# Own weight loads for some Q and K products, so that a group of four segments holds 4,096 TensorE instructions

## The chip, the cores and the metric

The kernel runs on one core of one Trainium2 chip. The metric is the device time of one execution in microseconds (us), as a median over several executions. TensorE executes the matrix products, and here it has two kinds of instruction: a matmul (PE in the profile) and the load of a weight block into the array (PEld). VectorE is DVE, ScalarE is ACT, GpSimd is POOL, and SyncE (SP) issues nearly all DMAs.

## The reference

Two independent branches are computed over 2,048 rows of width 640 and mixed by a gate. Branch A is attention with a recurrent memory: 64 segments of 32 rows, in which every segment sees 8 memory rows ahead of its own 32, and the first 8 output rows of a segment become the memory of the next one. Branch B is a gated MLP.

```python
for s in range(n_seg):                       # 64 segments, one after the other
    h = jnp.concatenate([mem, xs], axis=1)   # 8 + 32 rows
    q, k, v = (jnp.einsum('btd,dhe->bhte', h, W) for W in (Wq, Wk, Wv))   # 32 heads of 192
    p = softmax(where(mask, q @ k.T * scale, -1e9))
    o = jnp.einsum('bhte,hed->btd', p @ v, Wo)
    mem = o[:, :M, :]
    outs.append(o[:, M:, :])
b = (gelu(x @ w_gate) * (x @ w_up)) @ w_down
return g * a + (1 - g) * b                   # g = sigmoid(sum(x * gate_w))
```

(The loop's lines are shortened.) The last 8 rows of each segment can't reach the memory of the next one. The kernel calls them the left rows and computes them for four segments at once.

## The kernel before, in words

The kernel first runs branch B over four blocks of 512 rows (`ffn_gu`, `ffn_down`, lines 829 to 885) and stores its result to DRAM. It then computes the left rows' Q and K products for the first units (`left_mm`, line 917), and then the 64 segments (`segment`, line 1462).

Everything is recorded by a small scheduling layer (`_Sched`), which keeps one instruction list for each engine in the order of recording and puts in semaphore waits. The order within a segment is written by hand in three tables (`PROG`, `PROG1`, `PROG3`); a segment takes table `s % 4`, so the program repeats every four segments. Four segments are called a group; there are 16 groups. There is no loop in the machine program: all instructions are laid out one behind another, and each engine's list is fetched from DRAM while it runs.

A Q, K or V product of one segment (`proj`, line 1116) is done in octets of 8 heads and in 5 steps over the contraction (k = 0 to 4). One step of one octet is four matmuls: the stationary operand is the same 128x32 block of the segment's rows (`htile(k)`), and the four matmuls go to the four 32-column strips of the array (j = 0 to 3), each with 384 columns of the weight matrix as the moving operand. Where two or three products of one step stand behind one another they share that stationary block. So only the first of them loads it (line 1138, four weight loads and four matmuls); the others are issued with `ldweights=False` by `_matmul_kept` (line 226, four matmuls without a load). For the left rows, `left_mm` does the same: its Q product loads (line 930) and its K product keeps (line 226).

The other TensorE work of a segment: the scores (lines 1187 to 1202 and 234), the transposes of the probabilities (1249, 1254), the products with V (1282, 1284) and the output projection, in halves of 320 columns (1338), 160 columns for the last octet (1364), and 320 columns with 64 stationary columns in the fourth segment of a group (1383). The memory rows come back from the output projection through DVE: an add (line 1580) and two transposes (line 1583), for which the first K product of the next segment waits.

Of the kernel before, what the change touches and what calls it, by code (L numbers as in the profile page):

```python
# [223 lines left out]
def _matmul_kept(e, out, lhsT, rhs, like, stop):  # L224
    nm = e.bass.get_next_instruction_name()
    return e.add_instruction(mybir.InstMatmult(  # L226
        name=nm, start_tensor_calc=like["start"], stop_tensor_calc=stop, tile_size=(128, 32),
        tile_position=like["tile_position"], ldweights=False,
        ins=[e.lower_ap(rhs), e.lower_ap(lhsT)], outs=[e.lower_ap(out)]))
# [9 lines left out]
def _build(nc, A_x, A_mem0, A_Wq, A_Wk, A_Wv, A_Wo, seg_len, w_gate, w_up, w_down,  # L239
# [282 lines left out]
    def piece_view(key, o):  # L522
        if key[0] == 3:
            return bview(o, GO).rearrange("p (c n) -> p c n", n=Dm)
        return bview(o, GQ)
# [34 lines left out]
    def octet(s, i):  # L560
        return i if s % 2 == 0 else NOCT - 1 - i
# [5 lines left out]
    def group_at(item):  # L567
        return GROUPS[item[1]][::-1] if item[1:] == (0, 0) else GROUPS[item[1]]
# [69 lines left out]
    def piece(seg, key):  # L638
        order = orders[seg % 4]
        oi = last_req.get(seg, -1) + 1  # L640
        assert order[oi] == key, "pieces must be consumed in order"
        last_req[seg] = oi
        if seg == 0 and key in tmp_off:
            return left_piece(key)
        if seg and key == (EM, octet(seg, 0), EK):
            return None, None
        done_keys.append(key)
        return piece_view(key, res_off[key]), r_res[key]
# [164 lines left out]
    def htile(k):  # L813
        return XB[:, k, :]
# [98 lines left out]
    S_.add("pool", lambda e: e.memset(Qz, 0.0), writes=[r_Qz])  # L913
    lb = {}
    LBK = {}

    def left_mm(g, o, k, src):
        keys = [(m, o, k) for m in range(2)]
        for m, key in enumerate(keys):
            g_, rg_ = src(key)  # L920
            lhs = XLg[g % 2][:, k, :]
            fns = []
            for j in range(4):
                outp = ps[32 * j:32 * j + 32, LBK[m], 0:384].rearrange("p (c i) -> p c i", i=32)
                rhs = ek_j[j].rearrange("p (c i) -> p c i", i=32) if g_ is None else g_.rearrange("p (c j i) -> p j c i", c=12, j=4)[:, j]
                if m:
                    fns.append(lambda e, outp=outp, rhs=rhs, j=j: _matmul_kept(
                        e, outp, lhs, rhs, dict(start=(k == 0), tile_position=(0, 32 * j)), k == KT - 1))
                else:
                    fns.append(lambda e, outp=outp, rhs=rhs, j=j: e.matmul(  # L930
                        outp, lhs, rhs, start=(k == 0), stop=(k == KT - 1), tile_position=(0, 32 * j)))
            S_.add("pe", fns, reads=([rg_] if rg_ else r_ek) + [r_XLg[g % 2]], writes=[r_ps[LBK[m]]], name="L%s g%d o%d k%d" % ("QK"[m], g, o, k))

    def left_rows(g, o, m, bk, dst, rd, rowl, r_rowl):
        S_.add("act", lambda e: e.activation(out=rowl, in_=ps[:, bk, 0:384], func=ACTF.Copy),
               reads=[r_ps[bk]], writes=[r_rowl], name="L rows g%d o%d" % (g, o))
        S_.add("dve", lambda e: e.transpose(out=dst.rearrange("p q c i -> p c q i"), in_=rowl.rearrange("p (c r) -> p c r", r=L)),
               reads=[r_rowl], writes=rd, name="L T%s g%d o%d" % ("qk"[m], g, o))
# [20 lines left out]
    def vl_evac(s, o, bk, eng="dve"):  # L959
        out, in_ = vl_sb[o].rearrange("p (c n) -> p c n", c=3), ps[:, bk, 0:384].rearrange("p (n c) -> p c n", c=3)  # L960
        if eng == "act":
            S_.add("act", lambda e: e.activation(out=out, in_=in_, func=ACTF.Copy),
                   reads=[r_ps[bk]], writes=[r_vl[o]], name="Vl evac s%d o%d" % (s, o))
        else:
            S_.add("dve", lambda e: e.tensor_copy(out=out, in_=in_),
                   reads=[r_ps[bk]], writes=[r_vl[o]], name="Vl evac s%d o%d" % (s, o))
# [10 lines left out]
    for n, (g, o) in enumerate(units):  # L977
        b = n % 4
        for m in range(2):
            LBK[m] = ((3, 4), (0, 1), (2, 7))[n % 3][m]  # L980
        for k in range(KT):
            left_mm(g, o, k, left_piece)
        for m in range(2):
            left_rows(g, o, m, LBK[m], lst[b][:, :, m], [r_lst[b]], rows_sb[m], r_rows[m])
        if g == 0:
# [120 lines left out]
    def misc_bank(s, group=9):  # L1106
        tick[0] += 1
        ok = [b for b in (0, 1, 2, 3) + ((LB,) if s % 4 in (1, 2) or s % 4 == 3 and group < 3 else ()) + ((OB,) if group < (1, 3, 3, 9)[s % 4] else ()) if b not in bk_of.values() and b not in lb.values()]
        b = min(ok, key=lambda b: misc[b])
        misc[b] = tick[0]  # L1110
        return b
# [4 lines left out]
    def proj(s, item):  # L1116
        ms = GROUPS[item[1]]
        k = item[2]
        if k == 0:
            for mi in ms:  # L1120
                bk_of[mi] = LB if s % 4 == 0 and item[1] == 2 and mi[0] == 0 else misc_bank(s, item[1])
                if mi[0] == 2 and s % 4 == 0 and mi[1]:
                    bk_of[(3, mi[1])] = OB if mi[1] == 1 else LB

        def mms(m, bk, lhs, k, g_, keep):
            fns = []
            for j in range(4):
                outp = ps[32 * j:32 * j + 32, bk, 0:384]
                if m < 2:
                    outp = outp.rearrange("p (c i) -> p c i", i=32)  # L1130
                    rhs = ek_j[j].rearrange("p (c i) -> p c i", i=32) if g_ is None else g_.rearrange("p (c j i) -> p j c i", c=12, j=4)[:, j]
                else:
                    rhs = g_[:, 384 * j:384 * (j + 1)]
                if keep:
                    fns.append(lambda e, outp=outp, rhs=rhs, j=j: _matmul_kept(
                        e, outp, lhs, rhs, dict(start=(k == 0), tile_position=(0, 32 * j)), k == KT - 1))
                else:
                    fns.append(lambda e, outp=outp, rhs=rhs, j=j: e.matmul(  # L1138
                        outp, lhs, rhs, start=(k == 0), stop=(k == KT - 1), tile_position=(0, 32 * j)))
            return fns  # L1140

        for n, (m, i) in enumerate(group_at(item)):
            o, bk = octet(s, i), bk_of[(m, i)]
            g_, rg_ = piece(s, (m, o, k))
            S_.add("pe", mms(m, bk, htile(k), k, g_, n > 0),
                   reads=([rg_] if rg_ else r_ek) + [r_Hm[int(k >= KA[1])], r_HxT], writes=[r_ps[bk]],
                   name="%s s%d o%d k%d" % ("QKV"[m], s, o, k))
        for m, i in ms:
            if m == 2 and s % 4 == 0 and i:
                o, bk = octet(s, i), bk_of[(3, i)]  # L1150
                g_, rg_ = piece_view((2, o, k), res_off[(2, o, k)]), r_res[(2, o, k)]
                S_.add("pe", mms(2, bk, XLg[s // 4 % 2][:, k, :], k, g_, False),
                       reads=[rg_, r_XLg[s // 4 % 2]], writes=[r_ps[bk]], name="Vl s%d o%d k%d" % (s, o, k))
        if k < KT - 1:
            return
        for m, i in ms:
            o, bk = octet(s, i), bk_of[(m, i)]
            if m < 2:
                S_.add("act", lambda e, m=m, bk=bk: e.activation(out=rows_sb[m], in_=ps[:, bk, 0:384], func=ACTF.Copy),  # L1159
                       reads=[r_ps[bk]], writes=[r_rows[m]], name="rows evac")  # L1160
                continue
            S_.add("act", lambda e, i=i, bk=bk: e.activation(out=v_sb[i % NVB].rearrange("p (c n) -> p c n", c=3),  # L1162
                                                             in_=ps[:, bk, 0:384].rearrange("p (n c) -> p c n", c=3), func=ACTF.Copy),
                   reads=[r_ps[bk]], writes=[r_v[i % NVB]], name="V evac s%d o%d" % (s, o))
            if s % 4 == 0 and i:
                vl_evac(s, o, bk_of[(3, i)])
        tick[0] += 1
        for bk in bk_of.values():
            misc[bk] = tick[0]
        bk_of.clear()  # L1170
# [290 lines left out]

    def segment(s):
        g, q = s // 4, s % 4
        post = []
        n_wo, nqkv = n_wos[q], nqkvs[q]
        for n, item in enumerate(PROGS[q]):
# [24 lines left out]
            elif kind == "lf":  # L1491
                if i == q and unit(s, item[2]):
# [3 lines left out]
                    for m in range(2):  # L1496
                        LBK[m] = lb[item[2], m]
                    left_mm(*unit(s, item[2]), item[3], unit_piece)
# [97 lines left out]
    for s in range(NSEG):  # L1596
        segment(s)
# [79 lines left out]
```

## Time and profile before

| what | value |
|---|---|
| median of 3 runs | 1651.25 us (1649.93 to 1654.85) |
| span of the profiled execution | 2114.2 us; the page shows no time around the span |
| granted TensorE clock in the profiled execution | 0.654 of full speed, the same in all slices |
| TensorE matmuls | 37,107, busy 2098.0 us (99% of the span) |
| TensorE weight loads | 28,147, busy 958.1 us (45%) |
| DVE, ACT, POOL | busy 48%, 38%, 26% |
| DMA | 499.28 MB, mean 236 GB/s |

The profiled execution took longer than the timed runs: its span is 1.28 times their median. A line such as `L226 PE MATMUL ps<-arena ... x8960 | 887.8, 430 | 0.4` names the source line, the engine, the operation, output and input, the count, the busy time in us, the mean duration of one in ns, and the engine's idle time ahead of them. In the chain and in the timeline a row has its start in us, its length in us, and how many instructions were merged in it; matmuls on different strips of the array run at the same time, and a row's length in the chain is the step from one row to the next, while in the timeline it is from the first start to the last end. `arena` is the one tile in SBUF, and `ps` the one in PSUM.

### The profile page before, as it was taken

The numbers are of one execution on the slowest core, as the hardware profiler recorded it, in microseconds if no ns is written. First come the engines' busy times: TensorE is split into PE (matmuls) and PEld (weight loads), VectorE is DVE, ScalarE is ACT, GpSimd is POOL, SyncE is SP. The second block draws the span as 40 slices with busy tenths as digits, with TensorE's granted clock in tenths as the row PEclk, the third lists the DMA queues.
The fourth block names the chain that finished last, engine by engine and source line by source line (L and its number), as shares of the span: only waits on it lengthen the run. The fifth ranks groups of instructions, "written<-read, shape, count | busy, mean of one in ns | idle before, by whom it ended". The sixth has DMA issues, their size and how long they took to land.

```text
span 2114.2 us, 75845 instructions
## 1 busy us (share of the span) xinstructions
PE 2098.0 (99%) x37107; PEld 958.1 (45%) x28147; DVE 1005.8 (48%) x3039; ACT 792.9 (38%) x1890; POOL 553.3 (26%) x1625
## 2 busy tenths in 40 slices
PE   9999999999999999999999999999999999999997
PEld 3444344444444444444444444444444444444444
DVE  4233254554545454545545454545455454545453
ACT  1111244343434343444434343434444343434342
POOL 1000023232232223232222323232322223222332
PEclk6666666666666666666666666666666666666666
DMA  9612577776768777677767677776777676777775
GB/s 319 182 33 57 184 268 260 248 270 232 253 219 275 244 258 241 227 255 254 274 233 249 221 268 249 255 251 225 248 256 270 239 258 212 261 256 249 254 264 174
DMA packets 275415, 499.28 MB, mean 236 GB/s; under 512 B 121119, under 2 KB 136327, under 8 KB 275079
## 3 DMA queue, kind: packets, MB, share of 16 engines
q1 hardware_dynamic: 271000, 491.30, 68.8%
q8 instruction: 255, 4.18, 0.8%
q10 hardware_dynamic: 4079, 3.14, 0.5%
q14 instruction: 81, 0.66, 0.1%
HBM read 473.25 MB, written 21.09 MB: 234 GB/s over the span
## 4 chain that ended last, share of the span: by engine, by line
PE 99%; DMA 0%; DVE 0%; SPq 0%; POOL 0%; ACT 0%; issue 0%; ACTq 0%; POOLq 0%; DVEq 0%
PE ps L226 26%; PE ps L1138 25%; PE ps L1338 9%; PE ps L1383 8%; PE ps L1282 4%; PE ps L930 4%; PE ps L839 4%; PE ps L836 4%; PE ps L862 3%; PE ps L1364 3%; PE ps L1187 2%; PE ps L1284 2%; PE ps L234 1%; PE ps L1195 1%; PE ps L971 1%; PE ps L1254 1%
## 5 line engine op out<-in xcount | busy, mean ns | idle before, releaser
L226 PE MATMUL ps<-arena 128*32 128x384 bf16 x8960 | 887.8, 430 | 0.4 <-ACT arena L1159 0.4
L1138 PE MATMUL ps<-arena 128*32 128x384 bf16 x8640 | 857.5, 420 | 2.0 <-DVE arena L1583 2.0
L1138 PEld LDWEIGHTS ps<-arena 128*32 128x32 bf16 x8640 | 303.3, 117 | 525.3 <-issue 379.7
L1176 DVE STREAM_TRANSPOSE arena<-arena 128x384 bf16<-128x384 bf16 x512 | 276.5, 562 | 144.1 <-ACT arena L1159 144.1
L1159 ACT ACTIVATE arena<-ps 128x384 bf16<-128x384 f32 x512 | 230.0, 491 | 160.1 <-PE ps L1138 160.1
L1214 DVE TENSOR_REDUCE arena<-ps 104x4 f32<-104x160 f32 x256 | 83.0, 324 | 340.2 <-PE ps L1202 340.2
L1338 PE MATMUL ps<-arena 128*32 128x320 bf16 x3456 | 241.0, 404 | 0.0
L1012 POOL COPY arena<-arena 128x96 bf16<-128x96 bf16 x256 | 70.2, 274 | 475.3 <-PE ps L1202 311.4
L1267 ACT ACTIVATE arena<-ps 128x448 bf16<-128x448 f32 x192 | 104.4, 544 | 237.7 <-PE ps L1254 233.3
L1179 POOL COPY arena<-arena 64x160 bf16<-64x160 bf16 x256 | 81.9, 320 | 385.5 <-DVE arena L1176 384.3
L1162 ACT ACTIVATE arena<-ps 128x384 bf16<-128x384 f32 x256 | 125.2, 489 | 128.1 <-PE ps L1138 127.5
L1383 PE MATMUL ps<-arena 128*64 128x320 bf16 x1536 | 169.6, 387 | 0.0
L1226 ACT ACTIVATE ps<-ps 104x160 f32<-104x160 f32 x256 | 74.8, 292 | 239.5 <-DVE ps L1216 239.5
L1320 ACT ACTIVATE arena<-ps 128x480 bf16<-128x480 f32 x192 | 109.5, 570 | 93.8 <-PE ps L1284 85.7
L930 PE MATMUL ps<-arena 128*32 128x384 bf16 x1280 | 142.5, 408 | 0.0
L1338 PEld LDWEIGHTS ps<-arena 128*32 128x32 bf16 x3456 | 113.3, 129 | 56.9 <-ACT arena L1261 18.1
L1282 PE MATMUL ps<-arena 128*64 128x160 bf16 x1536 | 135.2, 263 | 0.0
L1284 PE MATMUL ps<-arena 128*64 128x64 bf16 x1536 | 128.6, 225 | 0.0
L1228 DVE TENSOR_REDUCE arena<-ps 104x4 f32<-104x160 f32 x256 | 81.8, 319 | 88.4 <-ACT ps L1226 87.4
L1383 PEld LDWEIGHTS ps<-arena 128*64 128x64 bf16 x1536 | 93.2, 127 | 49.4 <-issue 9.6
L1282 PEld LDWEIGHTS ps<-arena 128*64 128x64 bf16 x1536 | 94.1, 126 | 42.8 <-ACT arena L1159 23.0
L1411 ACT ACTIVATE arena<-ps 128x384 bf16<-128x384 f32 x120 | 57.3, 491 | 123.9 <-DVE arena L1580 74.0
(102 smaller groups left out, 2518.2 us busy)
## 6 DMA issues: line engine op xcount, KB each, us to landing
arena<-in_A_Wk_dram SPq DMA_DIRECT2D x335, 384.0 KB, 5.8
arena<-in_A_Wv_dram SPq DMA_DIRECT2D x335, 384.0 KB, 8.4
arena<-in_A_Wo_dram SPq DMA_DIRECT2D x205, 480.0 KB, 4.3
arena<-in_A_Wq_dram SPq DMA_DIRECT2D x209, 384.0 KB, 4.8
arena<-left_qk_scratch SPq DMA_DIRECT2D x126, 96.0 KB, 3.9
left_qk_scratch<-arena SPq DMA_DIRECT2D x49, 192.0 KB, 4.6
left_qk_scratch<-arena SPq DMA_DIRECT2D x30, 96.0 KB, 3.7
ffn_b_scratch<-arena ACTq DMA_DIRECT2D x16, 160.0 KB, 2.3
```

Of the source, the lines that this page charges most:

```text
L226: return e.add_instruction(mybir.InstMatmult(name=nm, start_tensor_calc=like["start"], stop_tensor_calc=stop, tile_size=(128, 32), tile_po ...
L930: fns.append(lambda e, outp=outp, rhs=rhs, j=j: e.matmul(outp, lhs, rhs, start=(k == 0), stop=(k == KT - 1), tile_position=(0, 32 * j)))
L1138: fns.append(lambda e, outp=outp, rhs=rhs, j=j: e.matmul(outp, lhs, rhs, start=(k == 0), stop=(k == KT - 1), tile_position=(0, 32 * j)))
L1159: S_.add("act", lambda e, m=m, bk=bk: e.activation(out=rows_sb[m], in_=ps[:, bk, 0:384], func=ACTF.Copy), reads=[r_ps[bk]], writes=[r_rows ...
L1162: S_.add("act", lambda e, i=i, bk=bk: e.activation(out=v_sb[i % NVB].rearrange("p (c n) -> p c n", c=3), in_=ps[:, bk, 0:384].rearrange("p ...
L1176: S_.add("dve", lambda e: e.transpose(out=dst[:, :, 0:L], in_=rows_sb[m].rearrange("p (c r) -> p c r", r=L)), reads=[r_rows[m]], writes=[r ...
L1267: S_.add("act", lambda e: e.activation(out=PT, in_=ps[:, bank, 0:PTW + 128], func=ACTF.Copy), reads=[r_ps[bank]], writes=[r_PT], name="pT ...
L1282: return [lambda e: e.matmul(full, v[:, e0:e0 + 64], PTm[:, i], start=True, stop=False, tile_position=(0, 64 * i), skip_group_check=True), ...
L1284: lambda e: e.matmul(part, vl[:, e0:e0 + 64], PTl[:, i], start=False, stop=True, tile_position=(0, 64 * i), skip_group_check=True)]
L1320: S_.add("act", lambda e: e.activation(out=apx(u[:, 0, 0, :], [[rs, na], [3 * rs, 4], [1, R]]), in_=ps[:, A, 0:na * W].rearrange("p (c t r ...
L1338: fns.append(lambda e, i=i, t=t, j=j, gv=gv: e.matmul(ps[32 * j:32 * j + 32, bank, 0:2 * DJ].rearrange("p (h n) -> p h n", h=2), lhs2[i], ...
L1383: S_.add("pe", [lambda e, i=i, g_=g_, c=c, p=p, u=u: e.matmul(ps[64 * i:64 * i + 64, LB, 0:2 * DJ], u[:, c, :], g_[:, c, 2 * DJ * i:2 * DJ ...
```

## The change

A counter `own` is set at the start of each segment to 34, 18, 0 or 74, by the segment's place in its group (112 more for the very first segment), and to 80 ahead of the left rows' first units. While it lasts, each matmul that would have kept the weights of its predecessor is issued with a weight load of its own, of the same block. Nothing else differs: the order of the matmuls, their operands, their semaphore waits and all other engines' instructions stay as they are. Where such a matmul has a wait, the wait stands at its load.

```diff
     lb = {}
     LBK = {}
+    OWN, OWN_PRE, OWN_FIRST = (34, 18, 0, 74), 80, 112
+    own = [OWN_PRE]
+
+    def own_load():
+        own[0] -= 1
+        return own[0] >= 0
...
     # left_mm
-                if m:
+                if m and not own_load():
                     fns.append(lambda e, outp=outp, rhs=rhs, j=j: _matmul_kept(
...
     # mms, in proj
-                if keep:
+                if keep and not own_load():
                     fns.append(lambda e, outp=outp, rhs=rhs, j=j: _matmul_kept(
...
     def segment(s):
         g, q = s // 4, s % 4
+        own[0] = OWN[q] + (OWN_FIRST if s == 0 else 0)
```

In a group, 34 + 18 + 0 + 74 = 126 loads are added. The program has 3,970 TensorE instructions in a group before (2,264 matmuls, 1,704 loads and 2 separate waits) and 4,096 = 16 x 256 in the change. The first segment has only 140 kept matmuls, fewer than its 146. So the whole program gets 80 + 140 + 18 + 74 + 15 x 126 = 2,202 more loads, 30,349 in place of 28,147. The lines of the changed file stand six (from line 936 on) to seven lines lower: 930 is 936, 1138 is 1144, 1187 is 1193, 1195 is 1201, 1202 is 1208.

The first place is TensorE's list at the start of the second group's first segment, where 34 loads are added. `L971` is the last product of the segment ahead, `L1138` a product with its own loads, `L226` one that keeps, and `L1187`, `L1195` and `L234` are the first scores. Before, from the third contraction step of the first product pair on:

```order
L1138 MATMUL ps<-arena 32x384 x4
L226 MATMUL ps<-arena 32x384 x4
L1138 MATMUL ps<-arena 32x384 x4
L226 MATMUL ps<-arena 32x384 x4
L1138 MATMUL ps<-arena 32x384 x4
L226 MATMUL ps<-arena 32x384 x8
L1138 MATMUL ps<-arena 32x384 x4
L226 MATMUL ps<-arena 32x384 x8
L1138 MATMUL ps<-arena 32x384 x4
L226 MATMUL ps<-arena 32x384 x8
L1187 MATMUL ps<-arena 40x160 x2
```

In the change, from the last product of the segment ahead to the same scores:

```order
L977 MATMUL ps<-arena 32x384 x20
L1144 MATMUL ps<-arena 32x384 x62
L226 MATMUL ps<-arena 32x384 x2
L1144 MATMUL ps<-arena 32x384 x4
L226 MATMUL ps<-arena 32x384 x8
L1193 MATMUL ps<-arena 40x160 x2
L1201 MATMUL ps<-arena 40x40 x8
```

The matmuls are the same ones in the same order. The first 62 all have loads, 34 of which are new, and keeping begins in the middle of a K product.

The second place is the start of a group's fourth segment, where 74 loads are added. Before, the end of the first product pair and the first steps of the next three products (V, Q, K) up to the scores:

```order
L1138 MATMUL ps<-arena 32x384 x4
L226 MATMUL ps<-arena 32x384 x4
L1138 MATMUL ps<-arena 32x384 x4
L226 MATMUL ps<-arena 32x384 x8
L1138 MATMUL ps<-arena 32x384 x4
L226 MATMUL ps<-arena 32x384 x8
L1138 MATMUL ps<-arena 32x384 x4
L226 MATMUL ps<-arena 32x384 x8
L1138 MATMUL ps<-arena 32x384 x4
L226 MATMUL ps<-arena 32x384 x8
L1187 MATMUL ps<-arena 40x160 x2
```

In the change, from the left rows' last products of the third segment (`L936`, `L226`) to behind those scores:

```order
L936 MATMUL ps<-arena 32x384 x4
L226 MATMUL ps<-arena 32x384 x4
L1144 MATMUL ps<-arena 32x384 x88
L1193 MATMUL ps<-arena 40x160 x2
L1201 MATMUL ps<-arena 40x40 x8
L234 MATMUL ps<-arena 40x40
```

All 88 matmuls ahead of the scores have loads of their own, so this stretch holds 176 instructions where it held 124, and the rest of the 74 follow behind the scores.

## The prediction

> **What bounds the kernel now.** I read the page's busy shares first, then TensorE's waits, then the chain, then four groups beside one another.
>
> ```profile
> span 2114.2 us, 75845 instructions
> ...
> PE 2098.0 (99%) x37107; PEld 958.1 (45%) x28147; DVE 1005.8 (48%) x3039; ACT 792.9 (38%) x1890; POOL 553.3 (26%) x1625
> ```
>
> ```profile
> core 0: 2114.2 us, clock 0.654
> ```
>
> ```profile
> PE ps L1202 <- POOL arena L1296: 6.3, 1, 6.3
> PE ps L1138 <- DVE arena L1583: 2.0, 3, 0.7
> PE ps L818 <- POOL arena L681: 1.4, 1, 1.4
> PE ps L1364 <- DVE arena L1314: 1.3, 3, 0.4
> PE ps L836 <- DMA arena<-in_B_w_gate_dram: 0.4, 1, 0.4
> PE ps L226 <- ACT arena L1159: 0.4, 1, 0.4
> PE ps L836 <- DVE arena L825: 0.2, 1, 0.2
> ```
>
> The page has matmuls under way for 99% of the span, the view of the cores has the granted clock, and the last view has all that TensorE waited for (total us, times, longest us). The 6.3 us fall once, in the last segment. The other rows add up to 5.7 us in 2114 us. So the span is TensorE's own work, at a granted clock of 0.654. How that work is paced is seen in the chain, within one segment (start us, step us, line, matmuls merged):
>
> ```profile
> 487.02 0.23 PE ps L1138 x4
> 487.26 0.23 PE ps L226 x4
> 487.49 0.23 PE ps L1138 x4
> 487.72 0.31 PE ps L226 x4
> 488.03 0.23 PE ps L1138 x4
> 488.26 0.23 PE ps L226 x4
> 488.50 0.23 PE ps L1138 x4
> 488.73 0.23 PE ps L226 x4
> ```
>
> L1138 is a product step with its own four loads, L226 one that keeps the weights. Both take 0.23 us; the one step of 0.31 belongs to a keeping one. So at this clock a step costs what its 384 columns take, and the loads lie under it.
>
> The timed runs are shorter than this execution: 1651.25 / 2114.2 = 0.781. If all time shrank with the clock, they had a clock of 0.654 / 0.781 = 0.84, and as waits don't shrink, it was between 0.84 and 1. I make the sum in the profile's microseconds and check each term at a full clock, where a step is 0.23 x 0.654 = 0.15 us. The result is given against the median.
>
> The instruction fetches have a DMA queue of their own (packets, MB, share of 16 engines):
>
> ```profile
> q8 instruction: 255, 4.18, 0.8%
> ```
>
> 37,107 + 28,147 = 65,254 TensorE instructions in 255 packets are 256 in each: this is TensorE's list, in blocks of 256 instructions and 4.18 MB / 255 = 16.4 KB. One packet takes 0.008 x 16 x 2114.2 us / 255 = 1.06 us.
>
> **The change part by part.** It adds 2,202 weight loads (126 in a group, more ahead of the first), removes nothing, and leaves the order of matmuls, the waits and the other engines alone. What can cost or gain is the loads, the waits that now stand at a load, the blocks, and where their borders fall.
>
> *The loads.* A step with added loads becomes what L1138 is, and the rows above show L1138 and L226 with the same step. Is there still cover at a faster clock? The densest stretch of loads tells:
>
> ```profile
> 1497.85 1.35 PE L1364 MATMUL ps<-arena 128*32 128x160 bf16 x46
> 1499.03 0.40 PE L930 MATMUL ps<-arena 128*32 128x384 bf16 x3
> 1499.04 0.37 PE L1364 MATMUL ps<-arena 128*32 128x160 bf16 x2
> ```
>
> These 48 matmuls of 160 columns have 48 loads. From their first start to the first start of the next product it is 1.18 us, so four matmuls with their four loads take 0.098 us, and one instruction 12.3 ns. A step of 384 columns takes 0.15 us even at a full clock, so four loads fit under it with a third of the time to spare. I take 0 us. The lower end is 0 too, since a load of weights that are there already can't shorten a matmul. The nearest upper end is that each load takes a place in the issue that nothing hides: 2,202 x 12.3 ns = 27 us. A further one is the loader's own busy time:
>
> ```profile
> L1138 PEld LDWEIGHTS ps<-arena 128*32 128x32 bf16 x8640 | 303.3, 117 | 525.3 <-issue 379.7
> L226 PE MATMUL ps<-arena 128*32 128x384 bf16 x8960 | 887.8, 430 | 0.4 <-ACT arena L1159 0.4
> ```
>
> 303.3 us / 8,640 = 35 ns a load, so 77 us if no load overlapped anything. The 379.7 us of idle time ahead of loads, in which they waited for nothing the profile shows, say that the loader has room: 77 us more bring it from 45% to 49%. I stay at 0, the row nearest to the case (L1138 against L226).
>
> One rule of the Trainium skill speaks against the change here. Its page "TensorE: Matmul & The Clock Gate", section "The mechanism", says that a load overlaps matmuls in flight only when it goes to another row group, and all of these products use all 128 rows. By that rule the sum would be +77 us. The trace doesn't agree: L1138 with its loads steps in 0.23 us, as L226 does without.
>
> *The waits.* Where a keeping matmul had a wait, its load now has it, and the matmul can follow only after the load. Of the 2,202, 35 wait for ACT (about two in a group) and 22 for others, mostly first DMAs. L226's row above has 0.4 us of idle time ahead of all its 8,960 matmuls, so practically none of these waits ends last. I take 0; if all 57 did, they would cost 57 x 117 ns (L1138's load) = 6.7 us.
>
> *The blocks.* 2,202 / 256 = 8.6 more packets of 16.4 KB are 0.14 MB in 499.28 MB: 0.
>
> *The borders.* Before, a group has 3,970 instructions, 15 blocks and 130 instructions, so from one group to the next the borders move by half a block against the program; in the change they stand at the same places in each group. If the place of a border mattered, neighbouring groups would differ. Four in a row, each from the same point of its program to the next:
>
> ```profile
> 481.88:597.87 115.99, 115.99 (x2268) 53.89 (x1706) 57.74 (x182) 47.05 (x116) 33.42 (x100) 0.65 0.73 248
> 597.87:713.87 116.00, 116.00 (x2268) 53.83 (x1706) 57.77 (x182) 47.06 (x116) 33.84 (x100) 0.65 0.74 248
> 713.87:829.86 115.99, 115.99 (x2268) 53.87 (x1706) 57.96 (x182) 47.05 (x116) 33.58 (x100) 0.65 0.73 248
> 829.86:945.85 115.99, 115.99 (x2268) 53.86 (x1706) 57.96 (x182) 47.05 (x116) 33.56 (x100) 0.65 0.73 248
> ```
>
> Each window holds the same 2,268 matmuls and 1,706 loads (those at its edges included) and is 115.99 or 116.00 us long. The borders moved three times, and the time moved by at most 0.01 us. So a border costs nothing at this clock, wherever it stands, and I take 0. What hides it is the work that TensorE has queued ahead. If that cover were gone at the faster clock, a border that stands where TensorE has just run dry could show one fetch, 1.06 us. With one such border in each of the 16 groups that is 17 us, to be gained if the old places were bad, or lost if one of the new ones is.
>
> The page "Runtime: NRT & Kernel Launch" of the Trainium skill, section "Instruction fetch mechanics", says the next block is fetched while the current one runs, and that crossing a border is mostly hidden. By it the placement gains nothing; the four windows agree.
>
> *The sum* is 0 + 0 + 0 + 0 on a span of 2114.2 us, and so 1651 us against the median.
>
> **The rivals.**
>
> *Borders do show at the timed clock, and the change takes them away (faster).* A clock of 0.84 to 1 leaves fewer nanoseconds of queued work, and a segment starts with a wait for DVE (L1583), behind which TensorE could run dry. For it speaks that the timed clock was not profiled; against it that this wait is only 2.0 us in three of 64 segments, and that the groups agree to 0.01 us. One border a group: 1651 - 17 = 1634 us. It decides from where TensorE's queued work at a border is shorter than the fetch.
>
> *Loads show at the timed clock (slower).* The place is the first 34, 18 or 74 kept matmuls of a segment, where eight instructions now stand under a step in place of four. At 12.3 ns each, 1651 + 27 = 1678 us. It decides from where a step gets shorter than four pairs of load and matmul, 0.098 us; a step at a full clock is 0.15 us, which speaks against it.
>
> *A fixed border stands at a bad place (slower).* What was a bad place in some groups is now one in all 16: 1651 + 17 = 1668 us. It decides on the same point as the first rival, and the same windows speak against it.
>
> *The change doesn't do what it says.* The program's count of a group is 4,096, so the blocks come out whole. Where the borders stand in the stretch depends on what is fetched ahead of the kernel's first instruction, which isn't shown. If they stand elsewhere, nothing is gained: within 1646 to 1656 us, as the forecast.
>
> **How the numbers follow.** A difference of 0.3%, 5 us, is about what a measurement of this kernel can tell from no change. The forecast, no change, gets 0.45, the case that the change misses its places included; its own range is 1646 to 1656 us. Borders gained get 0.30: the timed clock is higher than the profiled one, and that is the largest thing the profile can't show. Loads that cost get 0.14 and a bad fixed border 0.11, together 0.25 slower. The range goes from 1632 us, just past the first rival, to 1672 us, past the bad border and short of the full price of the loads: with both ends of what the borders may do in it, it leaves out about 1 in 10 on the slow side and somewhat less on the fast side, where more than one border in a group would have to show.
>
> **What would show it.** In the profile after, the loads are 30,349 and the packets of the instruction queue 263 or 264. Steps of the former L226 products with loads still take 0.23 us at a clock of 0.654, and the groups still take 115.99 us: then loads and borders are free at this clock. Groups that are longer by 126 x 12.3 ns = 1.5 us would show the loads. More idle time ahead of the new loads at L1144, ended by ACT, would show the waits. A timed median under 1646 us with unchanged groups in the profile would mean that the timed clock brings out something that this profile hides, and that is what would make the prediction wrong; if the profile after comes at another clock, its groups have to be compared with those of a run at the same clock.

## The result and the profile after

The change made the kernel slower by 0.4%: 1657.97 us (median of 22 runs, 1651.69 to 1664.92) against 1651.14 us (22 runs, 1642.29 to 1660.09), a ratio of 1.0038 with a 95% interval of 1.0025 to 1.0052. The time lies 2 us above the range of the forecast "no change" (1646 to 1656 us) and inside the wide one (1632 to 1672 us).

The profiled execution of the changed kernel ran at nearly the full TensorE clock, unlike the recorded one of the kernel before (0.654). So its page can't be laid beside that page, and the kernel before was profiled again: the experiment `e1_before`. The page, the view of the cores and the instruction queue of the changed kernel:

```profile
span 1655.9 us, 78030 instructions
...
PE 1563.2 (94%) x37090; PEld 830.4 (50%) x30349; DVE 996.4 (60%) x3039; ACT 785.9 (47%) x1890; POOL 549.5 (33%) x1625
...
PEclk9999999999999999999999999999999999999998
...
q1 hardware_dynamic: 271000, 491.30, 84.7%
q8 instruction: 263, 4.31, 1.0%
```

```profile
core 0: 1655.9 us, clock 0.997
```

The timed runs have this clock. Two shares have moved with it: matmuls fill 94% of the span, where they filled 99%, and the data queue (q1, share of the 16 DMA engines) takes 84.7%, where it took 68.8%. The line of the kernel before at the low clock, to be laid beside the one above:

```profile
q1 hardware_dynamic: 271000, 491.30, 68.8%
```

The same 491 MB go through in 0.78 of the time. The fetches of TensorE's list are 263, as forecast.

What TensorE waited for, in the changed kernel (total us, times, longest us):

```profile
PE ps L1260 <- issue: 13.4, 20, 1.0
PE ps L1370 <- issue: 10.9, 12, 1.7
PE ps L1208 <- POOL arena L1302: 7.8, 1, 7.8
PE ps L1208 <- issue: 7.6, 13, 1.1
PE ps L234 <- issue: 7.3, 12, 1.0
PE ps L1193 <- POOL arena L1185: 4.1, 17, 0.3
```

"issue" is time in which the engine waited for nothing that the profile shows. It was not in the recorded profile of the kernel before at all; here it is 43.4 us in 63 waits, over all rows of this view. Where it comes from can be seen in the timeline of the changed kernel, at the transposes of the probabilities:

```profile
308.08 0.22 PE L1260 MATMUL ps<-arena 104*32 104x128 bf16 x2
309.21 0.23 PE L1260 MATMUL ps<-arena 104*32 104x128 bf16 x2 [0.91 <-issue]
...
398.71 0.22 PE L1260 MATMUL ps<-arena 104*32 104x128 bf16 x2
399.58 0.23 PE L1260 MATMUL ps<-arena 104*32 104x128 bf16 x2 [0.65 <-issue]
...
488.82 0.22 PE L1260 MATMUL ps<-arena 104*32 104x128 bf16 x2
490.01 0.23 PE L1260 MATMUL ps<-arena 104*32 104x128 bf16 x2 [0.97 <-issue]
```

Four matmuls of one operation that share their wait stand still between the second and the third, for 0.65 to 0.97 us, some 90 us apart, which is one group. Counted from the program's first TensorE instruction (as number 0), the third of them is number 8,131, 12,227 and 16,323: each is a multiple of 256 plus 195. All 63 issue waits stand within two instructions of such a number. So they recur with the period of the fetched blocks, 256 instructions: these are the blocks' borders, and I read the waits as TensorE having run out of instructions. The experiments test that.

The step times say that the added loads are not what is slow. Mean durations (the second number after the bar, in ns) of products with loads (L1144) and without (L226) in the changed kernel:

```profile
L1144 PE MATMUL ps<-arena 128*32 128x384 bf16 x10742 | 663.9, 328 | 11.0 <-DVE arena L1590 2.3
L226 PE MATMUL ps<-arena 128*32 128x384 bf16 x6758 | 498.5, 326 | 3.6 <-issue 1.1
```

They differ by 2 ns. The ends of matmuls in a profile are modelled, so their starts are the better measure: from the first start of one step of four (384 columns each) to that of the next it is 0.163 us with loads and 0.162 us without (medians over the whole trace). And four groups, each from one point of the program to the same point in the next, as they were shown of the kernel before:

```profile
231.46:322.85 91.39, 87.27 (x2264) 46.68 (x1831) 57.29 (x182) 46.69 (x115) 33.43 (x99) 1.00 0.90 315
322.85:413.21 90.36, 87.17 (x2264) 46.50 (x1830) 57.12 (x181) 46.49 (x115) 33.38 (x99) 1.00 0.90 318
413.21:503.47 90.26, 86.81 (x2264) 46.70 (x1831) 57.08 (x182) 46.62 (x115) 33.38 (x99) 1.00 0.90 319
503.47:595.03 91.56, 87.22 (x2265) 46.46 (x1831) 57.19 (x181) 46.68 (x115) 33.31 (x99) 1.00 0.89 314
```

At the low clock the groups agreed to 0.01 us. Here they differ by up to 1.3 us, though in this kernel each group has its borders at the same places.

### The profile page after: what moved, and what is told of

The parts are those of the page before. It is cut to its first block, busy times and chain, and to the rows that moved or that the text cites. A ratio compares the mean times of both kernels' runs of the same rounds, so it can differ in the third digit from the quotient of the medians.

```text
span 1655.9 us, 78030 instructions
## 1 busy us (share of the span) xinstructions
PE 1563.2 (94%) x37090; PEld 830.4 (50%) x30349; DVE 996.4 (60%) x3039; ACT 785.9 (47%) x1890; POOL 549.5 (33%) x1625
## 3 DMA queue, kind: packets, MB, share of 16 engines
q1 hardware_dynamic: 271000, 491.30, 84.7%
## 4 chain that ended last, share of the span: by engine, by line
PE 71%; DMA 10%; DVE 8%; issue 4%; ACT 4%; SPq 1%; POOL 1%; DVEq 0%; ACTq 0%; POOLq 0%
PE ps L1144 23%; PE ps L226 12%; PE ps L1344 6%; PE ps L1389 5%; DMA arena<-in_A_Wo_dram 5%; DMA arena<-in_A_Wk_dram 3%; PE ps L936 3%; PE ps L1288 3%; PE ps L839 3%; PE ps L1193 3%; PE ps L836 3%; PE ps L1370 3%; PE ps L862 2%; PE ps L1201 1%; DVE arena L1182 1%
## 5 line engine op out<-in xcount | busy, mean ns | idle before, releaser
L1144 PE MATMUL ps<-arena 128*32 128x384 bf16 x10742 | 663.9, 328 | 11.0 <-DVE arena L1590 2.3
L226 PE MATMUL ps<-arena 128*32 128x384 bf16 x6758 | 498.5, 326 | 3.6 <-issue 1.1
L1144 PEld LDWEIGHTS ps<-arena 128*32 128x32 bf16 x10742 | 277.7, 96 | 332.7 <-issue 180.2
L1182 DVE STREAM_TRANSPOSE arena<-arena 128x384 bf16<-128x384 bf16 x512 | 272.3, 558 | 64.4 <-ACT arena L1165 63.5
L1344 PE MATMUL ps<-arena 128*32 128x320 bf16 x3456 | 181.7, 300 | 2.9 <-issue 0.4
L1018 POOL COPY arena<-arena 128x96 bf16<-128x96 bf16 x256 | 69.6, 272 | 260.7 <-PE ps L1208 171.9
L1389 PE MATMUL ps<-arena 128*64 128x320 bf16 x1536 | 123.0, 304 | 1.9 <-DMA arena<-in_A_Wo_dram 1.5
L1288 PE MATMUL ps<-arena 128*64 128x160 bf16 x1536 | 116.8, 240 | 3.4 <-ACT arena L1165 3.4
L936 PE MATMUL ps<-arena 128*32 128x384 bf16 x1380 | 110.5, 327 | 0.0
L1344 PEld LDWEIGHTS ps<-arena 128*32 128x32 bf16 x3456 | 86.5, 96 | 45.0 <-ACT arena L1267 18.5
L1334 POOL COPY arena<-arena 128x96 bf16<-128x96 bf16 x192 | 51.3, 267 | 160.7 <-ACT arena L1316 84.0
L1290 PE MATMUL ps<-arena 128*64 128x64 bf16 x1536 | 102.8, 193 | 1.8 <-issue 1.8
L1288 PEld LDWEIGHTS ps<-arena 128*64 128x64 bf16 x1536 | 81.3, 109 | 35.8 <-ACT arena L1168 14.4
```

What stands on the lines that cost most here:

```text
L226: return e.add_instruction(mybir.InstMatmult(name=nm, start_tensor_calc=like["start"], stop_tensor_calc=stop, tile_size=(128, 32), tile_po ...
L936: fns.append(lambda e, outp=outp, rhs=rhs, j=j: e.matmul(outp, lhs, rhs, start=(k == 0), stop=(k == KT - 1), tile_position=(0, 32 * j)))
L1144: fns.append(lambda e, outp=outp, rhs=rhs, j=j: e.matmul(outp, lhs, rhs, start=(k == 0), stop=(k == KT - 1), tile_position=(0, 32 * j)))
L1182: S_.add("dve", lambda e: e.transpose(out=dst[:, :, 0:L], in_=rows_sb[m].rearrange("p (c r) -> p c r", r=L)), reads=[r_rows[m]], writes=[r ...
L1288: return [lambda e: e.matmul(full, v[:, e0:e0 + 64], PTm[:, i], start=True, stop=False, tile_position=(0, 64 * i), skip_group_check=True), ...
L1290: lambda e: e.matmul(part, vl[:, e0:e0 + 64], PTl[:, i], start=False, stop=True, tile_position=(0, 64 * i), skip_group_check=True)]
```

## The experiments

Two theories stood against each other. **A, borders**: TensorE waits for the next block of its list, and the change moved the borders to worse places; the loads are free. **B, loads**: each added load costs TensorE about 3 ns (6.8 us / 2,202). A was later split: A1, the fetch is late because it stands behind the weight transfers; A2, the fetch takes that long by itself.

**The kernel before at the timed clock (`e1_before`).** No edit.

> The kernel before, unchanged, for a profile at the clock of the timed runs. The profile of the change has 263 block fetches and some 70 places where TensorE waits for the block, 50 of which the view of waits counts as issue (43 us in all). Theory A, borders: the kernel before has fewer or shorter such waits, in sum some 7 us less than the change, and the rest of a group takes the same time. Theory B, loads: the waits for blocks add up to the same within 3 us, and the change's steps with added loads are longer than the keeping steps of the kernel before, 7 us / 2,202 = 3 ns a load or 12 ns a step of four.

Its profiled execution took 1636.7 us at a clock of 0.996. That is one of this kernel's fastest (1638.56 us against a median of 1650.36 us of its runs on that chip), so its waits are probably at the low end, and the difference of the two profiles (19.2 us) overstates that of the medians (6.8 us). Its span, its data queue and its largest issue waits:

```profile
span 1636.7 us, 75845 instructions
...
q1 hardware_dynamic: 271000, 491.30, 85.4%
```

```profile
PE ps L1338 <- issue: 5.4, 13, 1.1
...
PE ps L1364 <- issue: 3.2, 4, 1.5
...
PE ps L1284 <- issue: 2.9, 4, 1.3
PE ps L1282 <- issue: 2.6, 3, 1.3
```

All rows together are 18.7 us in 30 waits, at seven lines, where the change has 57 of its 63 at four lines. That is A's picture: drifting borders meet many places, fixed ones the same few each time. The issue waits are 24.7 us less where A had guessed 7; a part of that belongs to the fast execution.

**All loads (`e2_all_loads`).**

```diff
-    OWN, OWN_PRE, OWN_FIRST = (34, 18, 0, 74), 80, 112
+    OWN, OWN_PRE, OWN_FIRST = (999, 999, 999, 999), 999, 0
```

> Every product that could keep its weights gets its own load: 37,107 loads, 8,960 more than before, and 290 blocks in place of 255. Theory B, loads cost 3 ns each: 8,960 x 3.1 ns = 28 us over before, about 1679 us. Theory A, only borders cost and the loads are free: 35 more borders at the mean wait per border that the change shows (43 us / 263 = 0.16 us) make 6 us, and with the borders drifting against the program again about 1657 us.

1715.77 us, a ratio of 1.0402 (1.0373 to 1.0431): 66 us by the ratio, more than either said. The waits of its profile:

```profile
PE ps L1144 <- issue: 30.5, 38, 1.9
PE ps L1344 <- issue: 16.2, 19, 1.7
PE ps L936 <- issue: 10.8, 10, 2.1
PE ps L1389 <- issue: 6.3, 7, 1.3
```

In all they are 88.7 us in 106 waits, 70.0 us more than in `e1_before`, while the span is 77.0 us longer (1713.7 us). So loads do cost, but as waits for blocks. My figure for A was too low because it took the mean wait per border as fixed. With more instructions in the same time a block lasts less long: 5.4 us from border to border (median, waits included) against 5.8 us in `e1_before`.

**Placement (`e3_shift128`, `e6_shift64`, `e7_shift186`, `e10_shift160`, `e8_plus40`).** The loads in the groups stay as in the change; only those ahead of the second group are varied, which moves all later borders against the program.

```diff
-    OWN, OWN_PRE, OWN_FIRST = (34, 18, 0, 74), 80, 112
+    OWN, OWN_PRE, OWN_FIRST = (34, 18, 0, 74), 16, 112   # e6_shift64
+    OWN, OWN_PRE, OWN_FIRST = (34, 18, 0, 74), 0, 58     # e3_shift128
+    OWN, OWN_PRE, OWN_FIRST = (34, 18, 0, 74), 0, 26     # e10_shift160
+    OWN, OWN_PRE, OWN_FIRST = (34, 18, 0, 74), 0, 0      # e7_shift186
...
-        own[0] = OWN[q] + (OWN_FIRST if s == 0 else 0)
+        own[0] = OWN[q] + (OWN_FIRST if s == 0 else 40 if s == 1 else 0)   # e8_plus40
```

> The change with 128 loads fewer ahead of the second segment (none ahead of the left rows' first units, 92 in the first segment in place of 140), so that all borders of the 16 groups fall 128 instructions later in the program. The loads within the groups are the same. Theory A: the waits for blocks move to other places, the sum of the waits named issue changes by 10 us or more from the change's 43 us, and the time moves with it, to either side of 1658 us. Theory B: 1658 us as the change, less 128 x 3 ns = 0.4 us.

> The change with 64 loads fewer ahead of the left rows' first units (16 in place of 80), so that all borders fall 64 instructions later in the program than in the change. A1 and A2: the sum of issue waits is again another than 43.4 us and 19.2 us, at other lines; the time is 1640 to 1675 us and goes with that sum. B: 1658 us.

> The change with no loads ahead of the left rows' first units and 34 in the first segment, so that the borders fall 186 instructions later than in the change. A1 and A2: again another sum of issue waits, with the time going with it, between 1640 and 1675 us; if the change's idea holds at all, one of the four placements tried (0, 64, 128, 186) is faster than the kernel before. B: 1658 us.

> The change with 160 loads fewer ahead of the second segment: borders 160 instructions later. By place: a ratio between 0.995 and 1.010, going with the sum of TensorE's waits; lying between the placements 128 (1.0017) and 186 (0.9970) it would be about 0.999 if the time changed evenly from one to the next, which nothing demands. By the number of loads: 1658 us.

> The change with 40 more loads, all in the second segment, so that from the third segment on all borders fall 40 instructions earlier in the program than in the change. By the placements so far (ratios to the kernel before: 1.0038 for the change, 1.0105, 1.0017 and 0.9970 for borders 64, 128 and 186 instructions later) place decides: the sum of all of TensorE's waits again goes with the time, and the ratio lies between 0.996 and 1.010. If instead the number of loads decides, it is the change's 1658 us.

| kernel | borders later by | ratio to before (95%) | issue waits, us | all TensorE waits, us | span, us |
|---|---|---|---|---|---|
| `e8_plus40` | -40 | 0.9920 (0.9891 to 0.9949) | 21.5 | 57.1 | 1636.4 |
| the change | 0 | 1.0038 (1.0025 to 1.0052) | 43.4 | 75.2 | 1655.9 |
| `e6_shift64` | 64 | 1.0105 (1.0071 to 1.0138) | 29.8 | 79.1 | 1664.4 |
| `e3_shift128` | 128 | 1.0017 (0.9994 to 1.0039) | 19.2 | 67.9 | 1655.0 |
| `e10_shift160` | 160 | 1.0030 (1.0009 to 1.0050) | 29.3 | 70.4 | 1652.9 |
| `e7_shift186` | 186 | 0.9970 (0.9947 to 0.9992) | 30.6 | 65.6 | 1647.3 |
| `e1_before` | drifting | 1 | 18.7 | 57.0 | 1636.7 |

The waits are sums over all rows of each profile's view. These kernels have almost the same loads (30,163 to 30,389), and they differ by 1.85%: place decides, and B falls. The interval of `e8_plus40` doesn't meet the change's; its ratio lies below the range that I had given (0.996 to 1.010). The sum of all waits roughly follows the span; issue waits alone do not (`e6_shift64` is the slowest with 29.8 us of them, and `e3_shift128` has few, but 12.7 us each behind DMA and ACT), so my expectation that the time goes with them was wrong. That a late block also makes what follows late would explain it, and is not shown. Against the kernel before, the places tried are worth from 0.8% less to 1.0% more, with a mean ratio of 1.0013. What fixed borders are worth by themselves stays open: all six placements also have some 2,000 loads more, and no run adds as many while the borders drift. From 128 to 186 the time doesn't change evenly. `e8_plus40`, at 1633.46 us, beats both kernels.

**Without the weight transfers (`e4_noswap_before`, `e5_noswap_after`, `e9_all_loads_noswap`).** The weight pieces that share a place in SBUF are exchanged again and again by DMAs that the code names "swap". These swap loads are left out of the kernel before, of the change, and of the kernel with all loads; from then on the products use wrong weights, but TensorE's instructions stay the same.

```diff
         loaded[slot_id[key]] = key
+        if name.startswith("swap"):
+            return
         S_.add("sp", lambda e: e.dma_start(piece_view(key, res_off[key]), piece_src(key)), writes=[r_res[key]],
```

> The kernel before with its swap loads left out (the weight pieces that share a place in SBUF are loaded once and not exchanged, so later segments use the wrong piece and the output isn't the reference's). Theory A1, the block fetch is late because it stands behind weight transfers: the waits named issue fall from 18.7 us to under 5 us, and the packets of the instruction queue start sooner after the border before theirs than the 2.0 us (median) of now. Theory A2, the fetch takes that long by itself: the waits stay at 15 to 22 us. Theory B says nothing of this kernel alone.

> The change with the same swap loads left out (same wrong pieces). A1: issue waits fall from 43.4 us to under 8 us, and its time is within 0.15% of the kernel before without swaps. A2: issue waits stay near 40 us, and it is 15 to 25 us slower in the profile than the kernel before without swaps. B, the loads cost TensorE time by themselves: the issue waits may go, but it stays 7 us slower than the kernel before without swaps.

> All 8,960 loads added, with the swap loads left out (later segments use the wrong pieces). If the 66 us that the same loads cost with swaps came only through block fetches that stand behind weight transfers, the time is that of the kernels without swaps, 1588 us within 3 us, with issue waits under 3 us. If loads cost TensorE anything by themselves, at 1 ns a load 9 us more, at 7 ns 66 us more.

1588.05, 1588.62 and 1589.24 us (ratios 0.9618, 0.9620 and 0.9643 to the kernel before with swaps, each within 0.0036). The change without swaps, its page, its data queue and its longest waits:

```profile
span 1586.1 us, 77123 instructions
...
q1 hardware_dynamic: 124696, 72.85, 16.6%
q8 instruction: 263, 4.31, 1.2%
```

```profile
PE ps L1203 <- DVE arena L1184: 4.0, 15, 0.3
PE ps L1195 <- POOL arena L1187: 3.4, 14, 0.3
PE ps L1290 <- ACT arena L1167: 3.4, 15, 0.2
```

The same 263 blocks are fetched, and the issue waits are 0.3, 0.7 and 0.6 us in the three kernels. So A1 holds and A2 falls. By these medians 2,202 loads cost 0.6 us and 8,960 cost 1.2 us (the latter run was on another chip) when no swap loads stand in the fetches' way, within the scatter of these runs (1586.9 to 1590.48 us): B falls a second time. From border to border it is 4.9 us in `e9_all_loads_noswap` against 5.6 us in `e4_noswap_before`, so blocks are shorter here too, and that alone costs next to nothing.

How late the fetch is can be worked out from the DMA packets of the instruction queue in the traces, set against the start of the matmul at the border before (the one numbered 195 plus a multiple of 256). With swaps the packet starts 2.0 us after it in `e1_before` and 2.6 us after it in the change (medians); without, about 0.3 us in both. It then takes 1.0 us, and where TensorE had waited, it went on 1.4 us after the end of the packet that had started in the block ahead. In the change, the packet started 3.4 us after the border ahead of those borders where TensorE waited, and 2.0 us ahead of the others. So a block of instructions was ready 3.4 + 1.0 + 1.4 = 5.8 us after the border in the one case and 4.4 us in the other, and a block lasts 5.7 us (median). In the recorded profile at the clock of 0.654 the packet started 0.7 us after the border, and a block lasted 7.4 us: there the fetch had room.

What stays open is why one place is better than another. Counted by its place in the group, one of the 16 borders waited in all six placements, for 6.7 to 16.4 us over the whole run, though it stood at L1208 in the change and at L1255 in `e10_shift160`. Another waited in all 16 groups of the change (L1260 and L1344, 12.2 us), and for 0.4 to 5.7 us in the other five placements. The swap loads are issued at fixed points of the program, so a place in the program is also a place among the transfers, and the runs don't part a place with little queued work from one with many transfers.

## Why the prediction was wrong

- **What bounds the kernel.** Right for the profile it was read from, and not for the timed runs. I had put their clock between 0.84 and 1; it is 0.997. Checking each term at a full clock, as I did for the loads, had to be done for the DMA too: 68.8% of the engines' time in the slow span is 85.4% in the fast one (`e1_before`).
- **The loads, 0 us: right.** 0.6 us for 2,202 of them without transfers, 1.2 us for 8,960. The step at a full clock, which I had at 0.15 us, is 0.163 us with loads. One reading was off: the 1.18 us of the densest stretch hold 46 matmuls and not 48, so four with their loads take 0.103 us in place of 0.098; nothing hangs on it. The rule of the Trainium skill that loads overlap matmuls only in another row group ("TensorE: Matmul & The Clock Gate", section "The mechanism"), by which the sum would have been 77 us more, doesn't hold in these runs either.
- **The waits at loads, 0 us: not seen to fail.** 5.6 us of TensorE's waits were ended by ACT in the change, 6.3 us in `e1_before`.
- **The blocks, 0 us: wrong in kind.** I counted the bytes of 8.6 more fetches. What matters is whether the fetch is done within the time that a block lasts. When all loads are added, a block lasts less long (4.9 us against 5.6 us without transfers), and with the transfers there are 70.0 us more of issue waits in a span that is 77.0 us longer. How much of the change's own 6.8 us comes from its 8.6 more blocks, and how much from their places, the runs don't part.
- **The borders, "a border costs nothing at this clock, wherever it stands, and I take 0": the step that failed.** The four equal groups showed it for a clock of 0.654 only, where a block lasts 7.4 us and its packet starts 0.7 us behind the border. At the timed clock, with the data queue at 84.7%, a block lasts 5.7 us and the packet starts at 2.6 us: 63 issue waits at the change's borders add up to 43.4 us, against 18.7 us in the profile of the kernel before, and moving the borders moves the time between ratios of 0.9920 and 1.0105. I knew that the cover was not shown for the faster clock, and gave both signs to it. The rival "a fixed border stands at a bad place", 1668 us at a chance of 0.11, is nearest to what happened. Its price, 1.06 us at one border a group, was the packet alone: the packet also starts 2.6 us late, and 57 of the 63 issue waits stand at four lines, with 0.6 to 0.9 us each on average. That the change came out only 6.8 us slower, and so near to the forecast, is luck of the place. The page "Runtime: NRT & Kernel Launch" of the Trainium skill, section "Instruction fetch mechanics", has a border mostly hidden. These runs agree where the DMA engines have room (0.7 us in `e5_noswap_after`); at 84.7% about a quarter of the borders, 63 of 263, were not hidden.
- **The first rival, borders gained (1634 us),** is a time that the same change gives at another place: `e8_plus40`, 1633.46 us. The mechanism is not the rival's: the waits are not taken away there, 21.5 us of them are left in 39 waits.

## What to carry to other kernels

A stall that an engine's queued work hides at one clock can be bare at another, so the clock and the DMA load of the profile have to be those of the timed runs before a wait is called free. A long unrolled program fetches its instructions through the same DMA engines as its data; where those are nearly full (85% here), look for waits named "issue" at equal distances, here of 256 instructions: they were late blocks. What moved them here was less traffic, the number of instructions in the time, and other places for the borders. A placement has to be tried on the chip in several positions before it is judged: here six of them lay 1.85% apart, on both sides of no change.

## What the runs showed of the hardware

TensorE's instruction fetch was one packet of 16 KB for every 256 instructions. It started about 0.3 us after the border before it without weight transfers, and 2.0 to 2.6 us after it with them (medians); as TensorE went on 1.4 us after that packet's end where it had waited, a block was asked for one block ahead here and not earlier. The scatter of the timed runs goes with the transfers too: 1638.47 to 1658.99 us over 17 runs of the kernel before, 1586.9 to 1590.48 us over 4 runs without them.
